# Cosine attention and a low-rank mixer on one core: the opening of batch 0 rearranged

## The chip, the cores and the metric

The kernel runs on one core of one Trainium2 chip. A core has a matrix engine (PE), a vector engine (VectorE, DVE in the profile), an activation engine (ScalarE, ACT), GpSimd (POOL), a queue engine (SyncE, SP) and sixteen DMA engines. Each engine carries out its own instructions in order and waits on semaphores for the others. The metric is the device time of one execution in microseconds.

## The reference

There are 8 batches, 12 heads, 448 positions and 64 columns per head, so 768 channels. The mixer's rank is 32 and its hidden width 3072.

```python
q_n = q / (norm(q, axis=-1) + 1e-6)
k_n = k / (norm(k, axis=-1) + 1e-6)
attn = softmax(q_n @ k_n.T / tau)
x = (attn @ v) as [8, 448, 768]          # heads side by side
xt = x.transpose(0, 2, 1)
u = x + (xt @ U @ V).transpose(0, 2, 1)
out = u + relu(u @ w_ch1) @ w_ch2
```

## The kernel before

**Layout.** A position is split into a row s of 112 and a part c of 4, so that a load of q or k brings rows of 1 KB to 112 partitions (`load_qk`, L379). Heads are worked in six pairs. For each pair the keys of head 0 go into the upper 64 columns of blocks of `xn` and those of head 1 into the lower 64, with zeros beside them, so that one product makes scores of one head from a 128-row operand. Blocks 0 to 7 of `xn` are keys, 8 to 11 are queries.

**Statistics.** `stats` squares q and k (L433 on ScalarE, L435 on VectorE), sums over 64 columns (L439), takes the norm as exp(0.5 ln) (L444, L447), adds epsilon (L450), inverts (L452), and `norm` multiplies (L474 for q, two calls of L477 for k). In batches 0 and 1 PE transposes `xn` (`flip`, L363) and ScalarE or VectorE copies the result to `qkT` (L732, L734). Later batches use DMA transposes on SP.

**Attention.** `attention` makes scores (L509), exponentials (L514), the product with V that carries a column of ones for the sum (L528), and divides (L535, L537) into `X_sb`. In batch 0 the keys are taken in 8 tiles of 112, and V comes as `raw_v` in that row order (`load_v0`, L410). In later batches there are 7 tiles of 128, the middle one shared by both heads, and V comes as `v_nat` in 14 pieces per batch (`load_v`, L401).

**Mixer.** `stage0` makes X·U (L585), and for batch 0 `columns` puts X and the V product together in a transposed form (L559, L564) as `uT`; six DMA transposes on SP (L601) bring it back as `u_nat`. Two batches share the seven 128-row tiles: batch 0, 2, ... take tiles 0 to 2, batch 1, 3, ... tiles 3 to 6. `mlp` then makes 24 chunks of the hidden layer with six products each (L681), applies relu (L691 on ScalarE, L693 on VectorE), and goes back with 24 products per half tile (L702). The first three half tiles of batch 0 are accumulated together: chunk after chunk, three products each. The second weight has the memory of `raw_v`; it is one buffer.

**Order of the work.** The program is not issued in the order of the code. `Plan.run` takes operations with a cost for each, keeps streams of PE and POOL in order and, at each step of an assumed time, gives every free engine the first ready operation: PE by the order of its streams (transposes first, then batch 0's scores, V products, low-rank products, other scores, MLP), ScalarE and VectorE by a priority. The result is a fixed order on each engine; at run time only semaphores count. Loads stand on POOL in the order in which the code creates them: batch 0's q, k and V, two quarters of `w_ch1`, q and k of batch 1 and the other two quarters in turns, V of batch 1, its last q and k, eight pieces of `w_ch2` (L348), and then batch 2. The loads of U and V stand on SP at the start (L768, L798).

**PSUM.** Three banks are shared by transposes and MLP (`r_mm`), three by scores (`r_sc`), two by V products (`r_av`).

Of the kernel before, what the change touches and what calls it, by code (L numbers as in the profile page):

```python
# [10 lines left out]
FP = mybir.dt.float32  # L11
# [38 lines left out]
class Plan:  # L50
# [4 lines left out]
    ENGINES = ("PE", "ACT", "DVE", "POOL", "SP")  # L55
    SEM = 0.10
    SAFE = 0.25
# [43 lines left out]
    def run(self):  # L101
        free = {e: 0.0 for e in self.ENGINES}
        dma = {"in": 0.0, "x": 0.0}
        heads = {e: [0] * len(s) for e, s in self.streams.items()}
        events = [0.0]
# [18 lines left out]
        while left:  # L124
# [6 lines left out]
            while progress:  # L131
                progress = False
                for e in self.ENGINES:
# [15 lines left out]
                    else:  # L149
                        w = known[e]  # L150
                        for i, (_, _, o) in enumerate(w):
# [10 lines left out]
                            heapq.heappush(events, r)  # L162
                        if pick is not None:
                            del w[i]
# [36 lines left out]
def kernel(  # L201
# [55 lines left out]
    r_ss = ring(2, [SCH, 2, G, SC], FP, "ss")  # L257
    r_ln = ring(2, [SCH, 2, G, SC], FP, "ln")
# [11 lines left out]
    w2, raw = Slot(r_w2, 1), Slot(r_w2, NPAIR)  # L270
# [22 lines left out]
    ident = const.tile([128, 128], BF, name="ident")  # L293
    w1_sb = const.tile([128, CC, F], BF, name="w1_sb")
# [15 lines left out]
    plan = Plan()  # L310
    pe_tp = plan.stream("PE")
# [19 lines left out]
    def load(fn, busy, deps=(), acq=(), rel=(), late=2.0):  # L331
        return plan.add(Op("POOL", 0.8, fn, deps=deps, acq=acq, rel=rel,
                           lat=("in", busy, late)), pool_q)
# [19 lines left out]
    def flip(stream, ins, n, into, part, deps, acq, rel, wide=1, eng="ACT/DVE"):  # L353
# [4 lines left out]
        for z, x in enumerate(ins):  # L358
# [6 lines left out]
            o = plan.add(Op("PE", 0.05, fn, deps=deps + [id_set] if z == 0 else (), acq=[tp] + acq,  # L365
# [7 lines left out]
    got = {}  # L373
    last_av = {}

    def load_qk(b, h0, h1, ld=None, lo=0):

        ld = ld or Slot(r_ld, 6)
        ops = [load(lambda i=i, src=src: nc.gpsimd.dma_start(  # L379
            out=ld.tile[:, i, lo:lo + h1 - h0, :],  # L380
            in_=src[b, h0:h1].rearrange("h (s c) d -> s h (c d)", c=SC)),
            (h1 - h0) * 0.5, acq=[ld], late=2.0 if b == 0 else LATE) for i, src in enumerate((q, k))]
        return ld, ops, lo

    def load_v(b, h0, h1):
# [3 lines left out]
        old = [v_set[b % 2]] + [last_av.get((b - 2, h // 2)) for h in range(h0, h1)]  # L389
        ops = []  # L390
        for hh in range(2):
            hs = slice(h0 + hh, h1, 2)
            for j in range(4):
# [4 lines left out]
                for n, c, s0, s1 in segments(lo, hi):  # L398
# [5 lines left out]
                        (s1 - s0) * (h1 - h0) * 0.001, deps=old, late=LATE))  # L404
# [3 lines left out]
    def load_v0(h0, h1):  # L408
# [4 lines left out]
            (h1 - h0) * 0.22, deps=[v0_set], acq=[raw]) for c in range(SC)]  # L413
# [3 lines left out]
    def stats(b, h0, h1, ld, ops, lo):  # L417

        g = h1 - h0
        pr = 0.3 + 0.03 * h0 if b == 0 else 4  # L420
        ss, ln, nv, inv = Slot(r_ss, 1), Slot(r_ln, 1), Slot(r_ln, 1), Slot(r_inv, 3 * g // 2)
        red = []
        for i in range(2):
            for a0 in range(0, g, G // 2):
                a1 = min(g, a0 + G // 2)
                sq = Slot(r_sq, 1)
                o = Op("ACT/DVE" if b == 0 and h0 < 4 else "ACT" if b == 0 else "DVE", any_t(256 * (a1 - a0), 2, 0.17), None,
                       deps=[ops[i]], acq=[sq], prio=pr + 0.2, fast=True)

                def square(o=o, i=i, a0=a0, a1=a1, sq=sq):  # L430
# [12 lines left out]
                    deps=[o], acq=[ss], rel=[sq], prio=pr + 0.1)))  # L443
        o = plan.add(Op("ACT", 0.25, lambda: nc.scalar.activation(  # L444
            ln.tile[:, :, 0:g, :], ss.tile[:, :, 0:g, :], AF.Ln),
            deps=red, acq=[ln], rel=[ss], prio=0))
        o = plan.add(Op("ACT", 0.2, lambda: nc.scalar.activation(  # L447
            nv.tile[:, :, 0:g, :], ln.tile[:, :, 0:g, :], AF.Exp, scale=0.5),
            deps=[o], acq=[nv], rel=[ln], prio=0))
        o = plan.add(Op("DVE", 0.21, lambda: nc.vector.tensor_scalar_add(  # L450
            nv.tile[:, :, 0:g, :], nv.tile[:, :, 0:g, :], EPS), deps=[o], prio=pr))
        o = plan.add(Op("DVE", 0.35, lambda: nc.vector.reciprocal(  # L452
            inv.tile[:, :, 0:g, :], nv.tile[:, :, 0:g, :]), deps=[o], acq=[inv], rel=[nv], prio=pr))
        for p in range(h0 // 2, h1 // 2):
            o_ = norm(b, p, ld, lo + 2 * p - h0, inv, 2 * p - h0, [o], pr)
        return o_

    count = [0]

    def norm(b, p, ld, la, inv, a, deps, pr):  # L460
# [3 lines left out]
        xn, qkT = Slot(r_xn, 2 if by_pe else 1), Slot(r_qkT, 8 if b == 0 else 7)  # L464
        deps = deps + [xn_set[count[0] % len(xn_t)]]
        count[0] += 1

        def part(i, hh):
            def fn():
                src = ld.tile[:, i, la:la + 2, :].rearrange("p h (c d) -> p h c d", d=D)  # L470
                sc = inv.tile[:, i, a:a + 2, :].unsqueeze(3)
                if i == 0:
                    dst = xn.tile[:, 8:12, :].rearrange("p c (h d) -> p h c d", h=2)
                    nc.vector.tensor_mul(dst, src, sc.to_broadcast([SCH, 2, SC, D]))  # L474
                else:
                    dst = xn.tile[:, 4 * hh:4 * hh + 4, 64 * hh:64 * hh + 64]
                    nc.vector.tensor_mul(dst, src[:, hh], sc[:, hh].to_broadcast([SCH, SC, D]))  # L477
            return plan.add(Op("DVE", dve_t(512 if i == 0 else 256), fn, deps=deps, acq=[xn],
                               rel=[ld, inv] if (i, hh) != (1, 0) else [ld, inv], prio=pr))

        ops = [part(1, 0), part(1, 1), part(0, 0)]
# [4 lines left out]
        else:  # L486
            done = []
            for b0, b1 in ((0, 8), (8, 12)):
# [3 lines left out]
                    ops, [qkT], [xn], 1, "ACT/DVE"))  # L492
        got[b, p, "qkT"] = (qkT, done)
# [3 lines left out]
    def attention(b, p, X):  # L497
# [4 lines left out]
        small = b == 0  # L502
        rows_ = SCH if small else 128
        for m in range(8 if small else 7):
            sc = Slot(r_sc, 1)

            def score(sc=sc, m=m):
# [4 lines left out]
            o = plan.add(Op("PE", pe_t(S), score, deps=qdeps, acq=[sc], rel=[qkT]),  # L512
                         pe_first if small else pe_sc)
            exps[m] = plan.add(Op("ACT", act_t(S), lambda sc=sc, m=m: nc.scalar.activation(  # L514
                out=attn.tile[0:rows_, m, off:off + S], in_=sc.tile[0:rows_, 0:S], func=AF.Exp,
                scale=inv_tau), deps=[o], acq=[attn], rel=[sc], prio=0.1 if b == 0 else 1))
        muls = []
# [365 lines left out]
```

## Time and profile before

| What | Value |
|---|---|
| median of three runs | 608.51 us (608.5 to 608.64) |
| profiled execution, its own time | 607.78 us |
| span of the profile | 605.9 us |
| PE busy | 585.8 us, 97% of the span |
| VectorE, ScalarE, POOL busy | 294.2, 282.4, 116.9 us |
| granted PE clock | full, in all slices |
| moved by DMA | 55.18 MB |
| chain that ended last | PE 91%, ScalarE 4%, VectorE 3%, DMA 1% |

The slices of the page cut the span into 40 parts of 15 us; a digit is a busy share in tenths. In lines of the timeline the first number is the start in microseconds from the begin of the span, the second the time covered, xN a count, and the bracket the idle time of the engine ahead of it and what ended that. "PE busy" joins overlapping products[...].

### The profile page before, as it was taken

The page shows a single profiled execution, that of the slowest core. Times are in us where ns is not written, and L with a number is a line of the kernel's source. Part 1 is how long each engine was busy: PE and PEld are TensorE (multiplying, and loading weights), DVE is VectorE, ACT ScalarE, POOL GpSimd, SP SyncE. Part 2 cuts the span into 40 slices and gives each one's busy share as a digit, 9 for nine tenths or more (in the row PEclk, how much of TensorE's full clock was granted, in tenths as well). Part 3 has the DMA queues.
Part 4 walks back from the last instruction along what each step waited for, and adds up shares of the span by engine and source line. Part 5 has one row for each costly group of instructions (what it writes and reads, how often), then busy time and mean ns, then how long its engine had stood idle before and what let it go on. Part 6 is the DMA issues. An engine that isn't in the chain of part 4 may idle for free.

```text
span 605.9 us, 11597 instructions
## 1 busy us (share of the span) xinstructions
PE 585.8 (97%) x4725; PEld 347.6 (57%) x4725; DVE 294.2 (49%) x756; ACT 282.4 (47%) x610; POOL 116.9 (19%) x178
## 2 busy tenths in 40 slices
PE   2899999999999999999999999999999999999997
PEld 1666666455565665666445665666545666654565
DVE  7976457989899899684811253015300210110011
ACT  4987524388863485327641077506442015014300
POOL 8525433026350615300600000000000000000000
PEclk9999999999999999999999999999999999999999
DMA  9999999679899999934932152030002110310021
GB/s 133 173 206 124 199 204 118 103 114 161 128 141 139 198 155 138 125 85 82 146 13 63 45 87 44 1 92 28 14 1 53 52 41 1 88 43 1 0 53 53
DMA packets 152725, 55.18 MB, mean 91 GB/s; under 512 B 117600, under 2 KB 152672, under 8 KB 152672
## 3 DMA queue, kind: packets, MB, share of 16 engines
q0 software_dynamic: 73408, 25.96, 39.7%
q1 hardware_dynamic: 79200, 28.45, 25.6%
q8 instruction: 37, 0.61, 0.4%
q14 instruction: 16, 0.13, 0.1%
q10 hardware_dynamic: 64, 0.02, 0.0%
HBM read 52.25 MB, written 11.01 MB: 104 GB/s over the span
## 4 chain that ended last, share of the span: by engine, by line
PE 91%; ACT 4%; DVE 3%; DMA 1%; POOL 0%; issue 0%; DVEq 0%; ACTq 0%; POOLq 0%
PE mm L681 36%; PE mm L702 35%; PE sc L509 10%; PE av L528 7%; ACT attn L514 3%; PE mm L620 1%; DMA qk_nat<-in_q_dram 1%; PE mm L585 1%; PE tp L363 1%; ACT sq L433 1%; DVE u_nat L634 1%; DVE O_sb L711 0%; POOL qk_nat L379 0%; DVE ss L439 0%; ACT qkT L732 0%
## 5 line engine op out<-in xcount | busy, mean ns | idle before, releaser
L702 PE MATMUL mm<-w_sb,relu 128*128 128x384 bf16 (+1 forms) x1368 | 238.0, 323 | 0.2 <-DVE O_sb L711 0.2
L681 PE MATMUL mm<-uT,w_sb 128*128 128x512 bf16 (+1 forms) x1152 | 234.8, 352 | 0.0
L514 ACT ACTIVATE attn<-sc 128x448 bf16<-128x448 f32 (+1 forms) x342 | 164.1, 563 | 82.2 <-PE av L528 51.9
L702 PEld LDWEIGHTS <-relu 128*128 128x128 bf16 x1368 | 132.5, 98 | 86.9 <-issue 0.8
L681 PEld LDWEIGHTS <-w_sb 128*128 128x128 bf16 x1152 | 112.3, 98 | 102.6 <-issue 0.8
L691 ACT ACTIVATE relu<-mm 128x512 bf16<-128x512 f32 (+1 forms) x175 | 95.4, 546 | 150.9 <-PE mm L681 150.8
L711 DVE TENSOR_TENSOR O_sb<-mm,u_nat 128x384 f32<-128x384 f32 (+1 forms) x57 | 31.1, 548 | 232.7 <-PE mm L702 229.1
L509 PE MATMUL sc<-qkT 128*128 128x448 bf16 (+1 forms) x342 | 103.7, 356 | 5.3 <-DVE qkT L734 2.5
L528 PEld LDWEIGHTS <-attn 128*128 128x128 bf16 (+1 forms) x1536 | 61.9, 98 | 16.8 <-DVE X_sb L537 0.8
L401 POOL DMA_DIRECT2D v_nat<-in_v_dram x98 | 63.5, 655 | 36.1 <-DMA w_sb<-in_moe_w_ch_dram 11.6
L439 DVE TENSOR_REDUCE ss<-sq 112x8 f32<-112x512 bf16 x96 | 63.0, 671 | 2.1 <-ACT sq L433 1.9
L528 PE MATMUL av<-v_nat,attn 128*128 128x65 bf16 x1344 | 55.8, 193 | 0.3 <-ACT attn L514 0.3
L379 POOL DMA_DIRECT2D qk_nat<-in_q_dram x25 | 17.9, 716 | 141.9 <-DVE xn L474 81.1
L509 PEld LDWEIGHTS <-qkT 128*128 128x128 bf16 (+1 forms) x342 | 31.5, 103 | 23.0 <-issue 5.7
L537 DVE TENSOR_TENSOR X_sb<-av,rd 128x256 bf16<-128x256 f32 x96 | 40.0, 416 | 1.3
L477 DVE TENSOR_TENSOR xn<-qk_nat,inv 112x256 bf16<-112x256 bf16 x96 | 36.9, 411 | 1.3 <-DMA qkT<-xn 1.1
L535 DVE RECIPROCAL rd<-av 128x4 f32<-128x4 f32 x96 | 16.8, 176 | 40.4 <-PE av L528 39.3
L435 DVE TENSOR_TENSOR sq<-qk_nat 112x512 bf16<-112x512 bf16 x85 | 32.7, 410 | 1.2 <-DMA qk_nat<-in_q_dram 1.2
L474 DVE TENSOR_TENSOR xn<-qk_nat,inv 112x512 bf16<-112x512 bf16 x48 | 32.7, 682 | 0.0
L634 DVE TENSOR_TENSOR u_nat<-mm,X_sb 128x384 bf16<-128x384 f32 x36 | 19.1, 549 | 10.0 <-PE mm L620 10.0
L363 PE MATMUL tp<-ident,xn 112*128 112x112 bf16 x144 | 10.4, 222 | 9.8 <-DVE xn L477 9.4
L379 POOL DMA_DIRECT2D qk_nat<-in_k_dram x25 | 17.6, 705 | 3.7 <-DMA w_sb<-in_moe_w_ch_dram 3.7
(56 smaller groups left out, 168.7 us busy)
## 6 DMA issues: line engine op xcount, KB each, us to landing
qk_nat<-in_q_dram POOLq DMA_DIRECT2D x23, 224.0 KB, 6.0
qk_nat<-in_k_dram POOLq DMA_DIRECT2D x23, 224.0 KB, 6.6
w_sb<-in_moe_w_ch_dram POOLq DMA_DIRECT2D x4, 1152.0 KB, 17.6
w_sb<-in_moe_w_ch_dram POOLq DMA_DIRECT2D x8, 576.0 KB, 15.3
out_dram<-O_sb SPq DMA_DIRECT2D x15, 168.0 KB, 2.4
out_dram<-O_sb SPq DMA_DIRECT2D x16, 144.0 KB, 2.1
out_dram<-O_sb SPq DMA_DIRECT2D x16, 120.0 KB, 1.9
out_dram<-O_sb SPq DMA_DIRECT2D x16, 96.0 KB, 2.2
```

What stands on the lines that cost most here:

```text
L379: ops = [load(lambda i=i, src=src: nc.gpsimd.dma_start(out=ld.tile[:, i, lo:lo + h1 - h0, :], in_=src[b, h0:h1].rearrange("h (s c) d -> s ...
L401: nc.gpsimd.dma_start(out=vb[p0:p0 + s1 - s0, hs, j, 0:D], in_=v[b, hs].rearrange("h (s c) d -> c s h d", c=SC)[c, s0:s1]),
L435: nc.vector.tensor_mul(y, x, x)
L439: lambda i=i, a0=a0, a1=a1, sq=sq: nc.vector.reduce_sum(ss.tile[:, i, a0:a1, :].rearrange("p h c -> p (h c)"), sq.tile[:, 0:a1 - a0, :].re ...
L477: nc.vector.tensor_mul(dst, src[:, hh], sc[:, hh].to_broadcast([SCH, SC, D]))
L509: nc.tensor.matmul(out=sc.tile[0:rows_, 0:S], lhsT=kT[:, rows_ * m:rows_ * (m + 1)], rhs=qkT.tile[:, 8:12, :].rearrange("p c s -> p (c s)" ...
L514: exps[m] = plan.add(Op("ACT", act_t(S), lambda sc=sc, m=m: nc.scalar.activation(out=attn.tile[0:rows_, m, off:off + S], in_=sc.tile[0:row ...
L528: nc.tensor.matmul(out=av.tile[:, t, 0:D + 1], lhsT=attn.tile[0:rows_, m, 128 * t:128 * (t + 1)], rhs=vv[0:rows_, h, j, 0:D + 1], start=(j ...
L537: muls.append(plan.add(Op("DVE", dve_t(256), lambda av=av, rd=rd, h=h: nc.vector.tensor_mul(X.tile[:, :, h * D:(h + 1) * D], av.tile[:, :, ...
L681: o = plan.add(Op("PE", pe_t(n), lambda f=f, cc=cc, mm=mm: nc.tensor.matmul(out=mm.tile[:, 0:n], lhsT=w1_sb[:, cc, f * 128:(f + 1) * 128], ...
L691: nc.scalar.activation(out=relu.tile[:, f, 0:n], in_=mm.tile[:, 0:n], func=AF.Relu)
L702: nc.tensor.matmul(out=mm.tile[:, 0:c1 - c0], lhsT=relu.tile[:, f, i * 128:(i + 1) * 128], rhs=w2.tile[:, f, c0:c1], start=(f == 0), stop= ...
```

## The change

For batch 0 the first pair goes its own way (`stats_first`): q's and k's statistics are made apart, q's square on VectorE and k's on ScalarE, and q, the keys of head 0 and the keys of head 1 are multiplied, transposed and copied one after the other. The statistics of heads 4 to 7 are made with PE (`squares_pe`): it transposes the raw data, ScalarE squares the result, and products with a two-column 0/1 matrix `pick` give the sums. Heads 4 to 7 and 8 to 11 have one set of statistics each instead of two. Only the first two pairs keep key tiles of 112 and `raw_v`; from the third pair on there are 7 tiles of 128, with V of heads 4 to 11 in 14 pieces. The six q and k loads of heads 0 to 7 come ahead of the identity matrix on POOL. U and V are loaded once the first pair's multiplications are done; their casts and the ones and zeros of `v_nat` move from VectorE to POOL, behind the first two quarters of `w_ch1`. Later pairs multiply k in one call. The first three MLP chunks of batch 0 use score banks, and five of their six products may begin before the last column block is there. Batch 1's squares wait for the last division of batch 0. The planner gets start times for the engines, a short look-ahead (`HOLD`) and other costs.

```diff
-    SEM = 0.10
+    BEGIN = {"PE": 1.0, "ACT": 2.0, "DVE": 0.9, "POOL": 1.3, "SP": 0.7}
+    SEM = 0.10
+    HOLD = 0.08
...
-        free = {e: 0.0 for e in self.ENGINES}
+        free = dict(self.BEGIN)
...
                             heapq.heappush(events, r)
+                            if r <= t + self.HOLD:
+                                break
...
+    pe_sum = plan.stream("PE")
+    pe_raw = plan.stream("PE")
     pe_tp = plan.stream("PE")
...
-    w2, raw = Slot(r_w2, 1), Slot(r_w2, NPAIR)
+    w2, raw = Slot(r_w2, 1), Slot(r_w2, 2)
...
+    def squares_pe(g, ld, ops, lo, ss, pr, hold):
+        for x in range(0, g, 2):
+            raw, sq = Slot(r_mm, 1), Slot(r_sqT, 1)
+            for y in range(8):
+                def flip_raw(y=y, x=x, raw=raw):
+                    nc.tensor.transpose(
+                        out=raw.tile[:, y, :], identity=ident[:SCH, :SCH],
+                        in_=ld.tile[:, y // 4, lo + x + y % 4 // 2, 128 * (y % 2):128 * (y % 2) + 128])
...
+            a = plan.add(Op("ACT", act_t(8 * SCH), lambda raw=raw, sq=sq: nc.scalar.activation(
+                out=sq.tile, in_=raw.tile, func=AF.Square), deps=[o], acq=[sq], rel=[raw], prio=pr + 0.2))
+            for y in range(8):
+                def add(y=y, x=x, sq=sq):
+                    nc.tensor.matmul(
+                        out=ss.tile[:, y // 4, x + y % 4 // 2, 2 * (y % 2):2 * (y % 2) + 2],
+                        lhsT=sq.tile[:, y, :], rhs=pick, start=True, stop=True)
...
+    def stats_first(ld, ops):
+        inv = Slot(r_inv, 3)
+        done, ups = {}, []
+        for i in range(2):
+            done[i], up = scales(0, 0, 2, ld, ops, 0, (i,), inv, -1 - 0.1 * i, ("DVE", "ACT")[i])
+            ups.append(up)
+        return ups + norm(0, 0, ld, 0, inv, 0, done, -1)
...
-        ops = [part(1, 0), part(1, 1), part(0, 0)]
+        if first:
+            ops = [part(0), part(1, 0, 1), part(1, 1, 2)]
+            blocks = [(8, 12, ops[0]), (0, 4, ops[1]), (4, 8, ops[2])]
+        else:
+            ops = [part(1), part(0)]
+            blocks = [(0, 8, ops[0]), (8, 12, ops[1])]
...
-        small = b == 0
+        small = b == 0 and p < 2
...
+        AHEAD = 3 if b == 0 else 1
...
+                    deps=([ut[cc], last_exp[0]] if b == 0 else ut if cc == 0 else []) + (
...
+                    early[g] = Slot(r_sc if b == 0 and f == 0 else r_mm, 1)
+                    if f == 0 and b == 0:
+                        up(g, early[g], range(CC - 1))
...
-        nc.vector.memset(t_[:, :, 0:3, D:D + 2], 1.0)
+        nc.gpsimd.memset(t_[:, :, 0:3, D:D + 2], 1.0)
...
-                    deps=[zf], prio=-2, lat=12.0)))
+                    deps=[zf, *begun], prio=-2, lat=12.0)))
...
-        nc.vector.tensor_copy(out=U_sb[:, par], in_=U_f()[:, par])
+        nc.gpsimd.tensor_copy(out=U_sb[:, par], in_=U_f()[:, par])
...
-        return stats(b, h0, h1, *load_qk(b, h0, h1))
+        return stats(b, h0, h1, *load_qk(b, h0, h1), hold=after if b == 1 else ())
...
+    first = load_qk(0, 0, 2, uses=5)
+    second = load_qk(0, 2, 4, first[0], 2)
+    ld, ops, _ = load_qk(0, 4, 8)
+    id_set = plan.add(Op("POOL", 0.8, lambda: make_identity(nc, ident)), pool_q)
+    begun = stats_first(*first[:2])
+    stats(0, 2, 4, *second, hold=begun)
     u0 = load_u(0)
...
+    stats(0, 4, 8, ld, ops, 0)
     load_v0(0, 4)
     ld, ops, _ = load_qk(0, 8, 12)
-    load_v0(4, 8)
-    load_v0(8, 12)
-    state[0] = att(0)
+    stats(0, 8, 12, ld, ops, 0)
+    load_v(0, 4, 12)
     w1_ops.append(load_w1(len(w1_ops), NW))
     w1_ops.append(load_w1(len(w1_ops), NW))
+    v_set = [plan.add(Op("POOL", 1.5, lambda t_=t_: set_v(t_)), pool_q) for t_ in v_t]
+    consts = [plan.add(Op("POOL", 0.4, lambda: cast_u(0), deps=u0 + [z], rel=[uv]), pool_q),
+              plan.add(Op("POOL", 1.2, cast_v, deps=v0 + [z], rel=[uv]), pool_q),
+              plan.add(Op("POOL", 0.4, lambda: cast_u(1), deps=u1 + [z], rel=[uv]), pool_q)]
+    state[0] = att(0)
+    after = last_mul[-1:]
     go(1, 0, 4)
```

## The prediction

> **What bounds the kernel now.** I read the page's forty slices first, then the timeline of the opening, then the table by stage, then the DMA queue.
>
> ```profile
> PE   2899999999999999999999999999999999999997
> DMA  9999999679899999934932152030002110310021
> ```
>
> PE is short of nine tenths in its first two slices only (15 us each); DMA is full for the first seven. So either the opening is shortened or nothing is. The timeline of the opening, all engines (start, duration, in brackets the idle time before it and what ended it):
>
> ```profile
> 9.38 1.49 PE L363 MATMUL tp<-ident,xn 112*128 112x112 bf16 x12 [9.38 <-DVE xn L477]
> ...
> 13.79 1.41 ACT L514 ACTIVATE attn<-sc 112x448 bf16<-112x448 f32 x3 [0.99 <-PE sc L509]
> ...
> 38.43 1.41 ACT L514 ACTIVATE attn<-sc 112x448 bf16<-112x448 f32 x3 [0.24 <-PE sc L509]
> ...
> 42.32 8.96 PE L681 MATMUL mm<-uT,w_sb 128*128 128x384 bf16 x54
> ...
> 83.06 7.49 PE L702 MATMUL mm<-w_sb,relu 128*128 128x384 bf16 x45
> ```
>
> First score 13.23, first exponential 13.79, last of batch 0 ends at 39.84; the MLP begins at 42.32. From then on PE is fed, by the table of busy time per stretch (time, PE busy):
>
> ```profile
> 42.30:88.90 46.60, 46.14 (x416) 29.50 (x415) 28.08 (x71) 27.16 (x60) 19.23 (x28) 1.00 1.28 177
> ```
>
> The five hundred microseconds behind it are as full, so whatever is gained at 42.32 is gained at the end, unless PE then overtakes its data. The data are the second thing to read: POOL issues nearly all loads, in one queue.
>
> ```profile
> 10.49 0.71 POOL L410 DMA_DIRECT2D raw_v<-in_v_dram  x1 [0.33 <-DMA qk_nat<-in_q_dram]
> 12.18 4.85 POOL L410 DMA_DIRECT2D raw_v<-in_v_dram  x7 [0.98 <-DMA qk_nat<-in_k_dram]
> 17.02 1.67 POOL L341 DMA_DIRECT2D w_sb<-in_moe_w_ch_dram  x2
> ...
> 50.95 0.62 POOL L401 DMA_DIRECT2D v_nat<-in_v_dram  x1 [7.19 <-issue]
> ...
> 57.07 0.72 POOL L379 DMA_DIRECT2D qk_nat<-in_q_dram  x1
> ...
> 58.47 6.13 POOL L348 DMA_DIRECT2D w_sb<-in_moe_w_ch_dram  x8
> ```
>
> Each load waits for the landing of the one eight places ahead (the code gives loads eight semaphores in turn): hence the waits at 10.49, 12.18 and 50.95. The answer for L348, the eight pieces of the second weight:
>
> ```profile
> L348 POOL DMA_DIRECT2D w_sb<-in_moe_w_ch_dram x8: 755/772/777, 58.5 to 63.8; - x8
> DMA to landing us min/median/max: 8.1/15.3/22.4
> ```
>
> The last piece lands at 63.8 + 22.4 = 86.2. Who uses it? The first group of down products takes three tiles per chunk, three chunks per piece, so piece 8 begins with product 64. The 45 products at 83.06 are numbers 28 to 72, (7.49 - 0.33)/44 = 0.163 us apart: number 64 starts at 83.06 + 36 x 0.163 = 88.93. **PE has only 88.93 - 86.2 = 2.7 us in hand over the weights.** Any gain above that, and any delay of the loads, meets there.
>
> **What the skill says.** "DMA: Bandwidth & Descriptors", section "SWDGE vs HWDGE vs iDMA": loads issued from GpSimd have descriptors written by that engine, DMA from SP goes into other internal queues, and each DMA engine takes turns between them. The trace agrees: between 44 and 46 us the SP queue's transposes and the weights pass 196 and 222 packets. "SBUF — State Buffer", section "SBUF: two separate sides": a VectorE operation in a two-port mode shuts GpSimd out for its whole length; no row here isolates that. "GPSIMD Engine Reference", section 3.1: an elementwise body costs 1.03 cycles per element, 1.2 GHz by section 1; used below. "Trainium Kernel Development and Optimization", section "Performance Expectations": matmul busy time is a poor measure; here too, one 384-column product shows 0.33 us but they follow each other at 0.163, so I count spacings.
>
> **The opening, step by step.** Loads: six q/k loads go first, identity (0.55 us on POOL) behind them at 5.5 to 6.0, needed at 7.9: hidden. VectorE's opening fills grow (third xn, second attn, pick), about 3.5 us of rows of 0.14 to 0.48 plus gaps, from 0.92 to 4.85: 0.3 later than the data (4.56). Then q square 0.42, two sums 0.69 each to 6.6, with q's ln and exp (0.2 each) under the second sum; q scale and product (0.17 + 0.25 + 0.69) to 7.8, k's (0.15 + 0.2 + 2 x 0.37) to 8.97. q's and k's first transposes and ScalarE copies end near 10.4, with one square (0.6) between the copies: first scores at 10.5 instead of 13.23. On PE 12 of the 16 raw transposes stand before those scores and wait for k of heads 4 to 7 (landed 11.9 before; with U and V out of the way I put it at 9.5; if 11.9, 1.5 us are lost here).
>
> ScalarE then goes without pause. First exponential 11.5, behind a 896-wide square (0.88, the row of the copy of that shape at 11.39). To the last one: 44 exponentials (4 fewer: pairs 2 to 5 use seven tiles) at 3.47/8 = 0.434 from the chain, 19.1; one more 896-wide square 0.9; three squares 1.8; five ln/exp 1.25; two 896-wide copies 1.6: 24.6, plus 0.5 where pair 2 waits for VectorE's products. End 36.6; before, 39.84. The MLP began 2.5 us later; its first products now need five column blocks, so 1.1 us of the last block's PE work comes after them: **MLP at 36.6 + 2.5 - 1.1 = 38.0, 4.3 us earlier.** By the order of instructions, PE then has what it had before up to product 64, plus that 1.1 us: 38.0 + 46.6 + 1.0 = 85.6, so 3.3 earlier than 88.93. The 16 raw transposes (0.06 each) and 16 two-column products (0.03, as the 65-column row, to 0.06) are 1.5 to 2 us where PE was idle 2.4 of 5 us; four scores less, 0.75.
>
> **The loads.** POOL: 1.28 + six q/k loads to 5.5, identity to 6.0, four V loads (0.70) to 8.8, two q/k to 10.2. Then V of eight heads in 14 pieces instead of 8 loads of 0.69. By rows of 0.52 for 16 rows x 6 heads, 0.77 for 112 x 6 and 0.70 for 112 x 4, the pieces cost 0.5 to 0.67, 8.25 in all. Unhindered the first weight load is issued at 18.5, which is 1.5 after 17.02 (1.3 us of waits fall away); the waits on heads 8 to 11 and on the 18 SP loads that now run from 9 to 17.5 may add 0 to 1.8 (later batches need 10.8 for 14 pieces). I take 19.4, **2.4 late**. From there the DMA is saturated (0.83 MB from 34 to 38 us, 208 GB/s) until the first weight has landed (24.7 + 25.2 = 49.9), so the delay is kept.
>
> Behind w1, POOL has ten memsets and three casts: 1776 + 704 elements on each partition at 1.03/1.2 ns, 2.1 us, plus 13 x 0.1 (the one-element memset): 3.4 us estimated, 2 to 7 if VectorE shuts it out. Queued behind them, and behind the casts' wait for U and V, are batch 1's loads. Two weights in the DMA queue hide it: the next load must be out near 31.5, and POOL is there at 24.5; past that each microsecond counts in full. They leave VectorE, where nobody waited for them. Uses are later too: V and its ones by pair 2 near 29, U and V by the first low-rank product near 33. The SP loads of U and V now wait for the first pair and land near 21.5; behind them on SP stand only the transposes, at 36.
>
> The six DMA transposes of u_nat (SP, 40.23 before) come 4 us earlier. They slow the weights: 170 against 208 GB/s from 44 to 46, 0.37 us for 196 packets. Of about 2300, 914 passed by 49.9; now I expect 1440, 0.5 to 1 us more on w1. But the V loads of batch 1 behind it then meet fewer: between 49.9 and 57.07 POOL was busy 4.5 of 7.2 us and waited for pieces slowed by 1576 transposes; with fewer, 5.5 to 6.2. Net -0.3 (-1.3 to +1).
>
> Last piece: 86.2 + 2.4 - 0.3 = 88.3, use 0.2 later, 88.5. PE, there at 85.6, **waits some 3 us for the weights**, at products 46 to 64. Result 88.5 - 88.93 = -0.4. Behind product 64 both orders hold the same 3962 matmuls. 607.78 (profiled execution, span 605.9) - 0.4 = 607.4; the median stands 0.73 above the profiled one: **608.1**.
>
> The rest at nothing: k's two products of later pairs become one (0.68 for 0.74, VectorE off the path); batch 1's statistics held to batch 0's last product (near 37.5; its loads land near 36 to 37 anyway); more buffers; three MLP tiles in score banks, free about ten microseconds before batch 1's scores. New planner costs act through the orders only.
>
> **Rivals.** *The loads are not late* (faster): if the transposes' relief takes back the POOL's delay, piece 8 lands near 86.4 and the gain is 2.3 (606.2); at most PE's own 3.3 (605.2). For it: V's tail has 2.7 us of waits to lose. Against: 8.25 us of issues for 5.5, a floor of 1.5. *The small V loads choke POOL* (slower): at the later batches' 10.8 us the first weight goes out at 21.0, piece 8 lands at 89.9 and PE is 1.2 behind, 609.7; at the 0.93 per piece seen from 85.6 to 98.6, 23.2, and 611.9. It decides once that issue is later than 21.0. *The opening does not shorten*, scores held by raw transposes and ScalarE: MLP at 42.3 gives 42.3 + 47.6 = 89.9, 609.5.
>
> **Numbers.** 0.2% (1.2 us) is about what a measurement of this kernel can tell from no change. The balance, 0.44, own range 607.3 to 609.5 (0.02 of the third rival in it); faster 0.28; slower 0.28, nearly all the second rival. Range 606.2 (first rival) to 610.9 (between the two paces of the second).
>
> **What would show it.** First score near 10.5, MLP near 38, first w1 issue between 18.5 and 21, V's tail (first weight landed to batch 1's last q load) under 7.2, PE idle before L702's counterpart on the w_sb DMA near 83 to 88. No such wait: the first rival. Wrong altogether would be a wait of PE in another place, as w1 late for the MLP (first piece due 29.6 against 38, third 43 against 53) or a planner's order that costs VectorE in batch 2.

## The result: slower, and where the time went

The changed kernel takes 612.48 us (median of four runs, 610.78 to 613.1) against 608.5 us: a ratio of 1.0062 (95% interval 1.0041 to 1.0083), 4 us slower. The forecast was 608.1, from 606.2 to 610.9. The profiled execution took 613.1 us (span 611.3; before 605.9), so it stands at the slow end of the runs shown, and its 5.3 us over the profiled execution of before are somewhat more than the 4 us of the medians.

The page of the changed kernel, its forty slices (15 us each, in tenths):

```profile
PE   3999978999999999999999999999999999999997
DMA  9999999879799999965932233041002110310021
```

The second slice is full now, which is the shorter opening. But slices 6 and 7 have fallen to 7 and 8 tenths: a hole between about 76 and 107 us that was not there before. The timeline of PE and ScalarE shows the opening and the hole (start, time covered, in brackets the idle time before it and what ended that):

```profile
10.44 0.55 PE L461 MATMUL raw<-ident,qk_nat 112*128 112x112 bf16 x4 [2.14 <-DMA qk_nat<-in_q_dram]
...
13.02 1.33 PE L579 MATMUL sc<-qkT 128*112 128x448 bf16 x3
...
13.63 0.54 ACT L584 ACTIVATE attn<-sc 112x448 bf16<-112x448 f32 x1
...
38.30 0.98 ACT L584 ACTIVATE attn<-sc 128x448 bf16<-128x448 f32 x2 [0.20 <-PE sc L579]
...
40.73 0.50 PE L754 MATMUL sc<-uT,w_sb 128*128 128x384 bf16 x2
...
80.73 3.59 PE L786 MATMUL mm<-w_sb,relu 128*128 128x384 bf16 x21
85.21 1.62 PE L786 MATMUL mm<-w_sb,relu 128*128 128x384 bf16 x9 [0.90 <-DMA w_sb<-in_moe_w_ch_dram]
88.02 1.62 PE L786 MATMUL mm<-w_sb,relu 128*128 128x384 bf16 x9 [1.19 <-DMA w_sb<-in_moe_w_ch_dram]
90.84 1.62 PE L786 MATMUL mm<-w_sb,relu 128*128 128x384 bf16 x9 [1.19 <-DMA w_sb<-in_moe_w_ch_dram]
93.83 1.62 PE L786 MATMUL mm<-w_sb,relu 128*128 128x384 bf16 x9 [1.36 <-DMA w_sb<-in_moe_w_ch_dram]
```

Four groups of nine products each wait for the piece of the second weight that they read. Product 64, the first to read piece 8, starts at 93.83; before it was 88.93. These 4.9 us are nearly all of the 5.4 us between the spans; the work behind product 64 takes 517.5 us, 0.5 more than before. The 21 products at 80.73 are numbers 16 to 36; at 0.163 apart PE without waits would have been at product 64 at 80.73 + 48 x 0.163 = 88.55. So **the opening gave PE 0.4 us at product 64, and the weights cost it 5.3, which leaves it 4.9 later than before.** The list of PE's waits says the same in one line (us in total, times, longest):

```profile
PE mm L786 <- DMA w_sb<-in_moe_w_ch_dram: 4.6, 4, 1.4
```

The queue of POOL, which issues the loads, shows why they are late:

```profile
10.68 0.70 POOL L409 DMA_DIRECT2D v_nat<-in_v_dram  x1 [0.51 <-DMA qk_nat<-in_q_dram]
12.16 2.92 POOL L409 DMA_DIRECT2D v_nat<-in_v_dram  x5 [0.78 <-DMA qk_nat<-in_k_dram]
15.28 0.62 POOL L409 DMA_DIRECT2D v_nat<-in_v_dram  x1 [0.20 <-issue]
16.50 4.23 POOL L409 DMA_DIRECT2D v_nat<-in_v_dram  x7 [0.60 <-DMA qk_nat<-in_k_dram]
20.72 1.68 POOL L349 DMA_DIRECT2D w_sb<-in_moe_w_ch_dram  x2
...
48.50 0.61 POOL L409 DMA_DIRECT2D v_nat<-in_v_dram  x1 [2.79 <-DMA qk_nat<-in_q_dram]
52.21 0.66 POOL L409 DMA_DIRECT2D v_nat<-in_v_dram  x1 [3.10 <-DMA qk_nat<-in_k_dram]
59.33 0.62 POOL L409 DMA_DIRECT2D v_nat<-in_v_dram  x1 [6.46 <-issue]
...
65.48 6.05 POOL L356 DMA_DIRECT2D w_sb<-in_moe_w_ch_dram  x8
```

The 14 V pieces of heads 4 to 11 take 8.47 us of issues and 2.09 of waits, so the first weight goes out at 20.72 (17.02 before). That is 3.7 us. The other half shows at 48.50 and 52.21: POOL waits there for q and k of batch 1's heads 4 to 7 to land, and then for the last quarter of the first weight. The eight pieces of the second weight go out 7.0 us later than before (58.47). The answer for L349, the four quarters of w1 (durations in ns, first and last start, then from issue to landing):

```profile
L349 POOL DMA_DIRECT2D w_sb<-in_moe_w_ch_dram x4: 842/846/847, 20.7 to 29.7; - x4
...
DMA to landing us min/median/max: 10.1/16.2/28.4
```

And that for L356, the eight pieces of w2:

```profile
L356 POOL DMA_DIRECT2D w_sb<-in_moe_w_ch_dram x8: 757/764/767, 65.5 to 70.8; - x8
...
DMA to landing us min/median/max: 8.4/15.6/23.0
```

Last quarter of w1: 29.7 + 28.4 = 58.1 (49.9 before); last piece of w2: 70.8 + 23.0 = 93.8 (86.26 before). In the trace's semaphore records, where each load lands in 16 parts, the delay of 7.5 us splits as follows.

| stretch | before | after | more |
|---|---|---|---|
| first issue of w1 | 17.02 | 20.72 | 3.70 |
| from there to the landing of its second quarter | 15.55 | 16.00 | 0.45 |
| second to fourth quarter of w1 | 17.34 | 21.42 | 4.08 |
| fourth quarter to piece 8 of w2 | 36.35 | 35.64 | -0.71 |

### The profile page after: what moved, and what is told of

Same layout as the page of the kernel before. It is cut to its first block, busy times and chain, and to the rows that moved or that the text cites. A ratio compares the mean times of both kernels' runs of the same rounds, so it can differ in the third digit from the quotient of the medians.

```text
span 611.3 us, 11591 instructions
## 1 busy us (share of the span) xinstructions
PE 589.1 (96%) x4753; PEld 350.0 (57%) x4753; DVE 304.0 (50%) x705; ACT 276.5 (45%) x591; POOL 123.1 (20%) x197
## 4 chain that ended last, share of the span: by engine, by line
PE 86%; DMA 5%; DVE 4%; ACT 2%; POOL 2%; issue 0%; DVEq 0%; POOLq 0%
PE mm L786 33%; PE mm L754 32%; PE sc L579 9%; PE av L599 7%; DMA w_sb<-in_moe_w_ch_dram 4%; ACT attn L584 1%; DVE ss L444 1%; DMA qk_nat<-in_k_dram 1%; PE mm L691 1%; DVE xn L542 1%; POOL w_sb L356 1%; PE tp L371 1%; POOL qk_nat L387 1%; PE mm L656 1%; DVE sq L440 1%; ACT qkT L816 0%
## 5 line engine op out<-in xcount | busy, mean ns | idle before, releaser
L584 ACT ACTIVATE attn<-sc 128x448 bf16<-128x448 f32 (+1 forms) x338 | 161.6, 554 | 81.5 <-PE av L599 49.9
L775 ACT ACTIVATE relu<-mm 128x512 bf16<-128x512 f32 (+1 forms) x163 | 89.0, 547 | 150.1 <-PE mm L754 149.8
L409 POOL DMA_DIRECT2D v_nat<-in_v_dram x112 | 71.8, 647 | 49.2 <-DMA w_sb<-in_moe_w_ch_dram 15.3
L599 PE MATMUL av<-v_nat,attn 128*128 128x65 bf16 x1472 | 62.4, 193 | 0.9 <-ACT attn L584 0.8
L542 DVE TENSOR_TENSOR xn<-qk_nat,inv 112x512 bf16<-112x512 bf16 (+1 forms) x97 | 62.0, 679 | 0.6
L440 DVE TENSOR_TENSOR sq<-qk_nat 112x512 bf16<-112x512 bf16 x87 | 35.9, 413 | 0.0
L371 PE MATMUL tp<-ident,xn 112*128 112x112 bf16 x144 | 11.9, 226 | 8.8 <-DVE xn L542 8.0
L777 DVE TENSOR_SCALAR relu<-mm 128x384 bf16<-128x384 f32 (+1 forms) x26 | 15.9, 610 | 3.8 <-PE mm L754 3.2
```

Source lines behind the costliest of these rows:

```text
L409: nc.gpsimd.dma_start(out=vb[p0:p0 + s1 - s0, hs, j, 0:D], in_=v[b, hs].rearrange("h (s c) d -> c s h d", c=SC)[c, s0:s1]),
L440: nc.vector.tensor_mul(y, x, x)
L542: nc.vector.tensor_mul(dst, src, sc)
L599: nc.tensor.matmul(out=av.tile[:, t, 0:D + 1], lhsT=attn.tile[0:rows_, m, 128 * t:128 * (t + 1)], rhs=vv[0:rows_, h, j, 0:D + 1], start=(j ...
L775: nc.scalar.activation(out=relu.tile[:, f, 0:n], in_=mm.tile[:, 0:n], func=AF.Relu)
```

## The experiments

Two questions: what made the third stretch 4 us longer, and why the opening gave PE 0.4 us instead of 3.3. For the first, my theory after the result was the six DMA transposes of `u_nat` on SP (L672). They start at 39.68, about when they did before (40.23), but the loads are 4 us later, so they now meet the third quarter (landing at 44.74), q and k of heads 4 to 7 (48.22, 51.92); before, these three landed at 40.51, 41.66 and 42.82. The rival was the loads' delay as such. All runs in one table. The ratios are to the kernel before of the same session, with 95% intervals; the last four columns are of one profiled execution each: when the first load of w1 is issued, the third stretch of the table above, when piece 8 of w2 lands, and when the MLP begins.

| kernel | median us | ratio | w1 issued | w1 quarter 2 to 4 | w2 piece 8 | MLP begins |
|---|---|---|---|---|---|---|
| before | 608.5 | | 17.02 | 17.34 | 86.26 | 42.32 |
| changed | 612.48 | 1.0062 [1.0041, 1.0083] | 20.72 | 21.42 | 93.78 | 40.73 |
| changed, no transposes | 607.71 | 0.9984 [0.9975, 0.9994] | 20.95 | 15.84 | 88.13 | 40.92 |
| before, no transposes | 608.38 | 1.0 [0.9991, 1.0009] | 17.29 | 16.19 | 85.48 | 42.91 |
| changed, transposes after w1's last quarter | 608.83 | 0.9995 [0.9985, 1.0005] | 20.06 | 16.16 | 88.07 | 39.19 |
| changed, transposes after k of heads 4 to 7 | 608.28 | 0.9996 [0.9987, 1.0005] | 20.88 | 16.92 | 89.40 | 40.92 |
| changed, transposes after w1's third quarter | 609.16 | 1.001 [1.0, 1.002] | 20.33 | 16.41 | 89.70 | 39.47 |
| before, loads of w1 delayed | 612.64 | 1.0073 [1.0057, 1.0089] | 21.64 | 20.53 | 93.66 | 43.39 |
| changed, V part undone | 610.62 | 1.0038 [1.0011, 1.0065] | 16.52 | 17.20 | 86.68 | 42.39 |
| changed, w1's first quarter ahead of V, late transposes | 609.35 | 1.002 [1.0009, 1.0031] | 10.16 | 17.09 | 88.26 | 39.91 |
| the same, raw transposes later | 607.07 | 0.9976 [0.9966, 0.9985] | 10.28 | 16.28 | 89.20 | 39.63 |
| changed, late transposes, raw transposes later | 606.73 | 0.9978 [0.997, 0.9986] | 20.31 | 15.47 | 88.12 | 39.43 |
| the same, casts of U and V later | 607.68 | 0.9985 [0.9975, 0.9996] | 20.85 | 15.88 | 88.58 | 38.79 |

Two cautions for reading the last columns. The profiled execution can be faster than the median: 607.31 for 608.83 with the transposes after w1's last quarter, 607.69 for 609.35 with w1's first quarter ahead of V. And five kernels have the same order of work on PE and ScalarE up to the MLP (the changed one, the one without transposes, the three with transposes after a load and no other edit), yet it begins between 39.19 and 40.92 in them, roughly in step with the landing of k of batch 0's heads 4 to 7 (10.45 to 11.99) and the first exponential (12.26 to 13.75). Differences of that size in the last column need not come from an edit.

**Without the six transposes**, in both kernels: VectorE fills `u_nat` with zeros instead, so the residual of batch 0 is left out.

```diff
-                nc.sync.dma_start_transpose(out=u_t[:, 0:3, cc * 128:(cc + 1) * 128], in_=uT.tile[:, cc, 0:384])
+                nc.vector.memset(u_t[:, 0:3, cc * 128:(cc + 1) * 128], 0.0)
```

> The changed kernel without the six DMA transposes of u_nat (VectorE fills u_nat with zeros in their place, so batch 0's residual is left out); the orders of PE, ScalarE and POOL stay as they are. Theory A (the transposes, 4 us earlier against a load stream 4 us later, hold up q/k of batch 1's heads 4 to 7 and the last quarter of w1): that quarter lands at 51.5 to 53.5 instead of 58.1, the last piece of w2 at 86.5 to 88.5 instead of 93.8, the waits of L702's counterpart for w_sb vanish or shrink under 1 us, and the span falls by 4.5 to 5.5 from 611.3. Theory B (the V pieces on POOL alone make w2 late, the transposes cost the same wherever they stand): last piece at 92 or later, span falls by under 1.5.

> The kernel before without the six DMA transposes of u_nat (zeros from VectorE, batch 0's residual left out), all other orders kept. Both theories: time within 0.6 us of before, because PE does not wait for w2 there. What it measures is what the transposes cost the loads at their old place: the last piece of w2 lands at 82.5 to 84.5 instead of 86.3 if they cost 2 to 4 us there, near 86 if nothing.

In the changed kernel the third stretch falls from 21.42 to 15.84 us, in the kernel before from 17.34 to 16.19. The transposes cost the loads 5.6 us in the one and 1.15 in the other. PE's wait for `w_sb` is gone and the changed kernel is now slightly faster than before, with the first weight still issued at 20.95. So the late issue alone doesn't make it slow.

**The transposes later.** A copy of 16 x 64 numbers on SP, which reads the last quarter of w1, stands ahead of them; the order of all other engines is that of the changed kernel.

```diff
+    gate = plan.add(Op("SP", 0.1, lambda: nc.sync.dma_start(
+        out=gate_sb, in_=w1_sb[0:16, 0, 3 * F // 4:3 * F // 4 + 64]), deps=[w1_ops[3]], prio=0, lat=2.0))
+    for o in got[0, "u"]:
+        o.deps.append(gate)
```

> The changed kernel with one small SP copy ahead of the six transposes that reads the last quarter of w1, so that they start only when it has landed; every other order is the same. Theory A: last quarter of w1 lands at 51.5 to 53.5, V's tail is 6.5 to 7.5 long, last piece of w2 at 88.5 to 90.5, span falls by 2.5 to 4.5 from 611.3. Theory B: last piece at 93 to 94.5, no gain.

All work is done, and the time is that of the kernel before. Of its twelve executions five took 607.0 to 607.5 us and seven 608.8 to 609.4; the profile is of one of the five. POOL's queue of this kernel, at the places of the two long waits above:

```profile
44.59 0.60 POOL L410 DMA_DIRECT2D v_nat<-in_v_dram  x1 [0.15 <-issue]
45.78 0.66 POOL L410 DMA_DIRECT2D v_nat<-in_v_dram  x1 [0.58 <-DMA qk_nat<-in_k_dram]
52.39 4.50 POOL L410 DMA_DIRECT2D v_nat<-in_v_dram  x7 [5.95 <-issue]
```

The waits of 2.79 and 3.10 for q and k have shrunk to 0.15 and 0.58. V's tail, which now meets the transposes, is not longer for it (from w1's landing at 51.20 to batch 1's last q at 56.87, 5.7 us; 5.9 in the changed kernel).

**The same delay in the kernel before.** Nine fills on POOL (4.27 us) ahead of the first load of w1, nothing else.

```diff
+    def pad():
+        for _ in range(9):
+            nc.gpsimd.memset(pad_t, 0.0)
+    plan.add(Op("POOL", 3.6, pad), pool_q)
     w1_ops.append(load_w1(len(w1_ops), NW))
```

> The kernel before with nine memsets (9 x 0.42 us) on POOL ahead of the first two quarters of w1, nothing else moved: the loads behind are 3.7 us late, PE is not. Theory A: the transposes now meet an earlier part of the stream, as in the changed kernel, so the last piece is later than 90, 91 to 94, and the time rises by 2 to 5 us. Theory B: the last piece lands 3.7 later, at 90.0, and the time rises by 1.0 to 1.4. If a late w2 did not matter the time would stay.

The old kernel with nothing but that delay is as slow as the changed one. POOL's queue:

```profile
21.64 1.66 POOL L341 DMA_DIRECT2D w_sb<-in_moe_w_ch_dram  x2
...
47.09 0.60 POOL L401 DMA_DIRECT2D v_nat<-in_v_dram  x1 [1.18 <-DMA qk_nat<-in_q_dram]
51.56 0.66 POOL L401 DMA_DIRECT2D v_nat<-in_v_dram  x1 [3.86 <-DMA qk_nat<-in_k_dram]
```

Weights issued 4.62 us later land 7.4 us later: the transposes (from 41.30 on) cost 20.53 - 16.19 = 4.3 us here. So neither the transposes nor the delay is enough alone; both together are.

**Which loads?** The gate was put on k of heads 4 to 7 (`in_=ld1.tile[0:16, 1, 3, 0:64]`), and on the third quarter of w1 (`in_=w1_sb[0:16, 0, 2 * F // 4:2 * F // 4 + 64]`).

> The changed kernel with a small SP copy ahead of the transposes that reads k of batch 1's heads 4 to 7, so that they start only when that load has landed (near 47), and so meet the last quarter of w1 and the V pieces only. If the q/k loads are what the transposes hold up (4 us of the 5.6): last quarter of w1 at 53.5 to 55, last piece of w2 at 88.5 to 91, span down by 2.5 to 4.5 from 611.3. If the weights suffer as much: last quarter after 56, last piece after 92, span down by less than 1.5.

> The changed kernel with a small SP copy ahead of the six transposes that waits for the third quarter of w1 instead of the last; the orders of all engines are those of the kernel with the gate on the last quarter. The transposes then start near 44.5 to 45.5, when one or two microseconds of the q and k loads of heads 4 to 7 of batch 1 are still to come, as in the kernel before (40.23 against landings of 41.66 and 42.82). If the cost comes from the pile of three loads (third quarter, q, k) that the transposes meet in the changed kernel, it falls to the 1 to 1.5 us of the kernel before: second quarter to last quarter of w1 17 to 17.6 us, piece 8 of w2 near 89, no more than one wait of PE for it, 608 to 609.5. If any overlap with q and k loads is enough, the q and k loads spread over more than 3 us again, second to last quarter takes 20 us or more, and the time is 611 or more.

Both stretches are short again: 16.92 with the transposes from 47.02 on, where only the last quarter of w1 is in flight, and 16.41 from 44.58 on, 0.4 us before q lands and 1.6 before k. Put in order by how long before the landing of the third quarter the transposes start, their cost against the run without them is: 5.06 us ahead, 5.6; 3.65 ahead (before, delayed), 4.3; 0.28 ahead (before), 1.15; 0.7 or more behind, 0.3 to 1.1. The kernel with the V part undone, shown next, adds a point without a partner of its own: 1.46 ahead, a stretch of 17.20, which is 1.0 to 1.4 over the two runs without transposes. Two later kernels with the transposes behind w1 have stretches of 15.47 and 15.88, so 0.4 us is within the spread of one kernel to the next. What is expensive in these runs is a start several microseconds before q and k of heads 4 to 7 land; 1.4 and 2.6 us ahead of them, as in the kernel before, it costs little. Whether the third quarter's tail must be there too, these runs don't separate.

**The V part undone**: all six pairs of batch 0 use tiles of 112 and `raw_v` again. PE's order is planned anew.

```diff
-    load_v(0, 4, 12)
+    load_v0(4, 8)
+    load_v0(8, 12)
```

> The changed kernel with its V part undone: all six pairs of batch 0 on tiles of 112, V of heads 4 to 11 in 8 loads as before. It tells how much of the 7.5 us came from the V pieces. w1's first load goes out near 17.3 instead of 20.7. Theory A (the collision with the transposes depends on where the stream stands when they start): the stream stands nearly as before, the transposes cost 1 to 3 us, last piece of w2 at 86 to 89, the MLP begins near 42 (four more exponentials), span 605.5 to 608. If the collision is the same as in the changed kernel in any case: last piece at 90, span 608 to 609.

The weights are on time again (issue 16.52, piece 8 at 86.68). PE does not wait for them, but this tells little: in the new order three pairs of batch 1 stand ahead of product 64 instead of two, and it starts at 99.29 only. The kernel is still slower than before. It has four exponentials more than the changed kernel and another order on PE, and the MLP begins at 42.39, where it began before the change. Without the V part the new opening gains PE nothing. How much of this is the exponentials and how much the order is open.

**w1's first quarter ahead of V**, with the late transposes, and in a second kernel with PE's transposes of the raw heads 4 to 7 behind the first pair's own.

```diff
     stats(0, 8, 12, ld, ops, 0)
-    load_v(0, 4, 12)
     w1_ops.append(load_w1(len(w1_ops), NW))
+    load_v(0, 4, 12)
     w1_ops.append(load_w1(len(w1_ops), NW))
```
```diff
-    stats(0, 4, 8, ld, ops, 0)
+    stats(0, 4, 8, ld, ops, 0, hold=[*got[0, 0, "qkT"][1](0), *got[0, 0, "qkT"][1](4)])
```

> The changed kernel with w1's first quarter issued ahead of the V pieces on POOL, so that it fills the DMA while POOL writes their descriptors, and the transposes held to the landing of w1's last quarter. Last quarter lands at 47 to 49, last piece of w2 at 82 to 85, no wait for w_sb on PE; what is left is PE's own opening (MLP at 40.7, 1.0 us more PE work than before): span 604.8 to 606.0, the time 0.1 to 1.2 us under before. If PE's opening were really 4 us shorter than before, 602 to 603.

> The kernel of the run before this with one more edit: the raw transposes of heads 4 to 7 come behind the first pair's copies, so that PE does not wait for the load of heads 4 to 7 ahead of the first scores. First scores at 10 to 11 instead of 13.0. If that wait is what the forecast of the opening missed: MLP at 38.5 to 39.5, span 602.5 to 604.3, 1.5 to 3.5 us under before. If ScalarE and VectorE are as late anyway: MLP after 40, span above 604.8.

The expected gain on the loads failed. The first quarter goes out 10 us earlier, but piece 8 lands at 88.26 and 89.20, no earlier than with the late transposes alone. A line of POOL's queue of the first of the two says why:

```profile
21.82 4.23 POOL L410 DMA_DIRECT2D v_nat<-in_v_dram  x7 [5.18 <-DMA w_sb<-in_moe_w_ch_dram]
```

The eighth load behind the quarter waits until that has landed, so V's other seven pieces and the second quarter (26.03) stand behind it: a load of 1.15 MB is a bad neighbour in a chain of eight semaphores. From 20 to 26 us the DMA moved 64 GB/s. The second kernel is faster than before; its other edit was then run without this one. The second kernel also has another order on PE: three pairs of batch 1 stand ahead of product 64, which starts at 97.48 (88.31 in the first kernel), so that PE needs piece 8 later. What that order is worth was not tried by itself.

**The raw transposes later, w1 as the change left it.**

> The changed kernel with two edits: the transposes of u_nat wait for the last quarter of w1, and PE's transposes of the raw q and k of heads 4 to 7 stand behind the first pair's own transposes and copies, so that the first scores don't wait for those loads. Loads of w1 stay where the change put them. My theory (PE's wait of 2.1 us for q of heads 4 to 7 delays the opening, but PE is then the full engine from 14 to 40 us and keeps most of the gain): first exponential near 10.6, last one of batch 0 ends near 38, MLP begins near 39.5, piece 8 of w2 near 88, time 606.5 to 608. Rival (the wait is the whole shortfall of the opening): the last exponential ends near 36, the MLP begins below 38.3, PE then waits over 1 us for w2.

It is 0.22% under the kernel before, level with the kernel just above (0.24%). Its ScalarE and PE:

```profile
10.56 0.53 ACT L585 ACTIVATE attn<-sc 112x448 bf16<-112x448 f32 x1
...
27.33 0.91 ACT L817 COPY qkT<-tp 128x896 bf16<-128x896 bf16 x1 [0.99 <-PE tp L372]
...
37.01 0.98 ACT L585 ACTIVATE attn<-sc 128x448 bf16<-128x448 f32 x2 [0.20 <-PE sc L580]
...
39.43 0.50 PE L755 MATMUL sc<-uT,w_sb 128*128 128x384 bf16 x2
```

The first exponential is 3 us earlier than in the changed kernel (13.63), the MLP only 1.3. Against the kernel with late transposes alone, on which this one is built, the exponential is 1.7 us earlier (12.26) and the MLP not at all (39.19): ScalarE's stream has grown from 25.49 to 27.43 us. Product 64 starts at 88.16 here and at 88.11 there, and the 0.7 us between the two profiled executions (606.64 and 607.31) lie behind it. So it is not shown that the earlier scores made the kernel faster. The numbers are those of my theory, its reason is not: PE was busy 9.37 of the 12 us from 14 to 26, VectorE 11.23 and ScalarE 10.92. One row of VectorE's timeline stands out:

```profile
18.41 0.17 DVE L497 TENSOR_SCALAR ln<-ln 112x32 f32<-112x32 f32 x1
...
24.08 1.48 DVE L497 TENSOR_SCALAR ln<-ln 112x32 f32<-112x32 f32 x1
```

Beside it runs the cast of V in POOL's timeline:

```profile
24.53 0.99 POOL L864 CAST V_sb<-raw_uv 128x448 bf16<-128x448 f32 x1
```

The same add of epsilon takes 0.17 at one time and 1.48 at the other, and then ends at 25.56, POOL's cast at 25.52.

**The casts behind w1's fourth quarter.** The last run tests that. PE, VectorE and ScalarE keep their orders.

```diff
     w1_ops.append(load_w1(len(w1_ops), NW))
+    for o in consts:
+        plan.add(o, pool_q)
     load_v(1, 0, 12)
```

> The changed kernel with the late transposes and the raw transposes behind the first pair, as before, and one more edit: the three casts of U and V on POOL stand behind the fourth quarter of w1 instead of ahead of batch 1's first loads. PE, VectorE and ScalarE keep the orders of that earlier kernel. There, VectorE's add of epsilon on 112x32 numbers took 1.48 us at 24.08 instead of 0.17 and ended within 0.04 us of POOL's cast of V; PE's transposes of the last pairs then waited 1.1 us. Theory (the cast on POOL holds the add back): the add takes 0.17, PE's wait of 1.1 for xn near 26.7 goes, the MLP begins 0.5 to 1.3 earlier (38.1 to 38.9); the time gains less, 605.9 to 606.7, since piece 8 of w2 still lands near 88 and PE waits for it. Rival (the add is late for another reason, as its input from ScalarE): the add is as long as before or starts later, and the MLP begins at 39.4 again.

The same add in this kernel:

```profile
24.57 0.34 DVE L497 TENSOR_SCALAR ln<-ln 112x32 f32<-112x32 f32 x1
```

And PE's timeline, the first product of the MLP and product 64:

```profile
38.79 0.50 PE L755 MATMUL sc<-uT,w_sb 128*128 128x384 bf16 x2
...
88.62 1.62 PE L787 MATMUL mm<-w_sb,relu 128*128 128x384 bf16 x9 [1.19 <-DMA w_sb<-in_moe_w_ch_dram]
```

The add is down to 0.34 (it now meets a fill on POOL that ends at 24.87), PE's wait of 1.1 for `xn` is gone, and the MLP begins at 38.79, the earliest of all. The time did not follow, 607.68: piece 8 landed at 88.58, and PE waited 1.19 for it instead of 0.34. The opening is no longer what decides; the weights are.

## Why the prediction was wrong, step by step

**The balance was the right mechanism.** PE runs into the second weight at product 64, the waits stand at products 37 to 64 (46 to 64 forecast) on the `w_sb` DMA, and what lies behind takes 0.5 us more. Three terms were off.

1. **"Net -0.3 (-1.3 to +1)" for the transposes is the step that failed**, and the only one outside its own bounds by much. It was 4.08 - 0.71 = +3.4 us. The count was off: 2173 of the transposes' 2496 packets (not 2300) passed before w1 had landed, where I expected 1440; before the change it was 918. The price was off too: at the forecast's 0.37 us for 196 packets the 1255 more make 2.4 us, not 4.08. I had counted the transposes' packets as if the sixteen DMA engines were one pipe: so many packets more on w1, so many fewer on V. The trace doesn't behave so: k of heads 4 to 7 landed its 16 parts between 45.46 and 51.92, where without transposes they lay within 2.0 us (45.24 to 47.27), and POOL waits for the last part. The Trainium skill, "DMA: Bandwidth & Descriptors", section "SWDGE vs HWDGE vs iDMA", which I had drawn on, says that each engine takes turns between queues; how far one engine may fall behind another is what this trace shows. I had also noted that the transposes come earlier, when the loads are later, and had not asked which loads they would then meet.
2. **"2.4 late" for the first weight was 3.7.** The V pieces were costed well (8.47 us for 8.25); the waits between them were 2.09 where I took 0.9 and had bounded them at 1.8. A further 0.45 came before the second quarter landed.
3. **"MLP at 38.0" was 40.73**, and PE without waits at product 64 at 88.55 instead of 85.6. The length of ScalarE's stream was right: 25.65 us from the first exponential to the end of the last one, 25.1 forecast. Its start was wrong, 13.63 for 11.5: the raw transposes stand ahead of the first scores and waited 2.14 us for q of heads 4 to 7, which landed at 10.39. I had put k at 9.5, "with U and V out of the way"; it landed at 11.88, before the change at 11.90. But U and V were not out of the way:

```profile
3.83 3.35 SPq L854 DMA_DIRECT2D raw_uv<-in_moe_U_dram  x7
...
8.35 0.76 DVE L542 TENSOR_TENSOR xn<-qk_nat,inv 112x256 bf16<-112x256 bf16 x2
```

   SP issues their loads from 3.83 us on, just behind the fill of `raw_uv` (3.53 to 3.80) and well before the first pair's last multiplications (8.35 to 9.11). The dependency on these stands in the planner's time alone; at run time nothing makes SP wait for them. So "U and V are loaded once the first pair's multiplications are done" was not so, and what k would do without them was not run. The sentence "if 11.9, 1.5 us are lost here" was the better half of that step. With PE's wait taken away (the run with raw transposes later) the stream starts at 10.56, but lasts until 37.99, since ScalarE then waits twice for PE (1.03 and 0.99 us), which waits for VectorE (0.76 and 1.11). The second of these went when the casts were moved. A smaller slip: the last block's work behind the exponentials is 1.1 us in the words of the forecast, 1.0 in its sum, and 1.2 in the trace (47.8 us from the first product of the MLP to product 64 without waits, 46.6 before).

With 1.3 us from term 2, 0.45 behind it and 3.7 from term 1, product 64 comes 5.3 us later than the 88.5 of the forecast (the sum is 5.4; the use follows the landing by 0.05, not 0.2). Term 3 cost nothing in the end, as PE would have waited anyway; but with it most of the gain was gone too, and with the transposes out of the way the time is that of the kernel before.

Right were V's tail (5.93 us, 5.5 to 6.2 forecast), the fills and casts on POOL (3.7 us, 3.4 estimated, hidden from the loads as said; the large fills took 0.42 us each, 0.44 by the forecast's price, but the cast of V 0.97, 0.48 by the same price) and, within 0.5 us, the work behind product 64. Of the rivals, "the small V loads choke POOL" comes nearest in time, 609.7 to 611.9, but not in its condition: it was to decide once the first issue is later than 21.0, and 20.72 isn't, and with the same issue and later transposes the loss is gone. "The opening does not shorten" held in part, and by the cause it names: the raw transposes held the first scores until 13.02 (13.23 before), and PE without waits is at product 64 only 0.4 us earlier; but the MLP began 1.6 us earlier. "The loads are not late" is out.

## What to carry to other kernels

When a change delays a stream of loads, list what else uses the DMA engines at fixed times and ask which loads it will meet now; a collision may cost as much again as the delay itself (4.1 us on top of 3.7 here), and holding the lesser transfer back behind the stream by one small gated copy gave 3.7 us of time back (612.48 to 608.83). Where PE waits for data in an order written out by hand, put work that needs a later load behind the work that doesn't, and look how far the gain gets: here the first exponential came 1.7 us earlier and the MLP did not. A dependency that only a planner knows orders the issue and nothing more: look in the trace whether the wait is there. And before shortening a stage, find the next thing that PE meets: the earliest opening here (MLP at 38.79) did not give the best time, because the weights came at 88.

## What the runs showed of the hardware

- **Six SBUF-to-SBUF DMA transposes cost a stream of loads on another queue 4.3 and 5.6 us in two kernels, 0.3 to 1.15 in four others**, depending on when they start. In the changed kernel one load's 16 parts land up to 6.5 us apart (2.0 without the transposes), and the DMA moved 157 GB/s from 44 to 48 us, where it moved 211 with the transposes held back. Why an engine that falls behind doesn't recover is not shown.
- **A small VectorE operation can wait out a GpSimd one.** The add on 112 x 32 float32 numbers took 1.48, 1.26 and 0.79 us in three kernels where it met GpSimd's cast of V (0.99 to 1.00), ending within 0.05 us of it; with the cast moved it took 0.34. Where the same add did not meet that cast, it took 0.17 us at the least (w1 early, raw transposes later) and 0.44 at the most (V part undone), so only what is above some 0.4 us is put down to the cast. The Trainium skill, "SBUF — State Buffer", section "SBUF: two separate sides", says that of a VectorE operation in a two-port mode and a GpSimd one, whichever starts first holds the shared pair of ports for its whole instruction; I had priced only VectorE shutting GpSimd out. The ends of the three adds look like the other side of that rule. Two of these rows begin 0.2 and 0.5 us before the cast's own, while GpSimd was at a fill or another cast, so how the ports pass from one to the next is not shown.
